# A fused attention and feed-forward kernel: TensorE's run on a pair broken in two places by feed-forward work, the weights' floor on ScalarE and GpSimd, the first values copied out of PSUM, and new orders

## The chip, the cores and the metric

The kernel runs on one core of a Trainium2 chip. The metric is the device time of one execution in microseconds. Three executions of the kernel before took 775.16, 775.26 and 775.63 us (median 775.26).

## What is computed

`reference()` does an attention with a cumulative bias and then a gated feed-forward layer, for 8 batches, 8 heads, 576 positions and a head width of 64:

```
scores = q @ k.T / 8 + min(cum[key] - cum[query], 0)        # cum = cumsum(max(s, 0)); causal
attn   = exp(scores - max);  attn /= sum(attn) + 1e-9
x      = attn @ v, heads side by side                        # 8 x 576 x 512
h      = relu(x @ w_in)                                      # 512 -> 1024
gate   = sigmoid(conv of three taps over positions of h)     # conv_w: 3 x 1024
out    = (h * gate) @ w_out                                  # 1024 -> 512
```

q, k, v and s are 32-bit floats; `w_in`, `conv_w` and `w_out` come as 64-bit floats and are turned into 32-bit ones on the chip, by integer work on their two words.

## The kernel before

**Pairs.** The 64 heads are handled as 32 pairs p, two heads in the two halves of the 128 partitions; four pairs make a batch. A pair's work, by the names of the tasks in the code:

- `qk`, `v`: loads. `hi`, `lo`: the operands are split into a rounded 32-bit part (`hi`, ScalarE or VectorE) and the rest (`lo`, GpSimd or VectorE), so that three products give nearly full precision.
- `sh0` to `sh3` (L1038): a first product of scores on TensorE, in four parts, each into two PSUM banks; `mx` (L1060, L1069): VectorE takes their row maxima. For late pairs (p >= 7) the bias comes through rows `rw` that GpSimd cuts (L996). `tn` (L1089), `rt`, `ds`: the maxima are turned and sent by DMA to the row that serves as shift.
- `sc0` to `sc3` (L1156): the scores proper, four parts, two banks each; `ex` (L1175): ScalarE takes the exponential (by a sigmoid with an offset) out of PSUM into `pt`; `mk` (L1187): GpSimd cuts the diagonal blocks.
- `sum` (L1269): the row sums by a product with ones (from p = 9 on, after additions `ad` on VectorE and GpSimd); `pv` (L1212): the product with the values, into the one PSUM tile `pv` (two banks).
- `gd`, `fo`, `inv`, `ri`, `rb` (L1288 to L1316): the sums are folded over the partitions by a DMA, inverted on VectorE, stored to DRAM and read back spread over the partitions into `rb`. `nm` (L1324): VectorE multiplies the PSUM tile `pv` by `rb`; by that the tile comes free for the next pair's `pv`. `xh`, `xl`: the result is split again and kept as `x`.

**Feed-forward work**, for each batch in two halves of the positions (256 and 320): `h` (L1376, 12 matmuls for each of 8 columns of `w_in`, one bank), `re`, `ce`, `ta`, `tb`, `ga`, `mu` (ScalarE and VectorE), `uh`, `ul` (split into `u`), and `o` (L1505, six matmuls for each fourth of an output block, whose bank is held over the four), `oe`, `st`.

**PSUM** has eight banks: two for `pv` and six (`ps`) for everything else.

**Weights.** `weight_piece` (L742 and on) loads 8 pieces of `w_in` and 4 of `w_out` with 512 columns, 8 of `w_out` with 256, and `conv_w` with 24. The wide ones use three sets of buffers `w` of their own, the others the feed-forward buffers `ht` and `ct`, of which there are three each. A piece goes through these steps: `load`; `one` (L774, VectorE: low part of the high word, shifted); `square` (L781, ScalarE: the square of the high word read as a float, into a buffer of its own); `two` (L785, VectorE: sign and top exponent bit); `both` (L791, VectorE: bits of the low word); `three` (L799, VectorE: multiplies by 0 where the square is too small); `h` and `l`, the split into `wi` or `wo`.

**The order.** All instructions of all engines are put in order on the host before the launch. `Sched.play` simulates the engines with a duration per task (the numbers in `add(...)`), a DMA rate, waits and buffers, and at each moment lets an engine take the ready task with the lowest tag. A tag is a due time from the task's place in the pair plus a number from the table `DUE`. TensorE prefers tasks of the mode that it is in (by 4 us of tag), since a change of mode has a cost in the simulation. The order that comes out is fixed in the program; at run time each engine works it off and waits where something isn't ready. SyncE issues all DMAs.

**Bursts.** From pair 9 (`B0`) on, the TensorE tasks around a pair form a burst: `ORDER` lists them, `group()` gives those that belong together one number, and while a burst is open TensorE takes no other task. In the kernel before, the whole list is one burst: `sh0`, `sh1` of the next pair, `sum`, `pv` of the previous one, `sh2` of the next, `sc0`, `sc1` of this one, `sh3`, `sc2`, `sc3`. `link()` chains the tasks in this order and lets the first task of a part wait for all that its part needs. A "|" in `ORDER` begins a new part.

Of the kernel before, what the change touches and what calls it, by code (L numbers as in the profile page):

```python
# [1623 lines left out]
```

## Time and profile before

| | |
|---|---|
| median of three executions | 775.26 us (775.16 to 775.63) |
| the profiled execution | 780.03 us, of which 778.1 us are its span |
| granted TensorE clock, mean | 0.987 of full speed |
| busy: TensorE, VectorE, ScalarE, GpSimd | 729.7, 568.5, 445.5, 350.4 us |
| DMA | 75.15 MB, mean 97 GB/s |

The span runs from the first to the last instruction. Busy time of TensorE holds the time of a matmul record even where the array waits inside it, and the records overlap; so a stage is better read from the starts of its instructions. The granted clock has two levels here, 1.2 and 2.4 GHz, shown as 0.50 and 1.00 of full speed; a value between them is a stretch that holds both.

### The profile page before, as it was taken

To read this page: it belongs to the slowest core of one execution; us is meant where nothing else is said; L and a number is where in the kernel's file an instruction comes from. 1 tells how busy PE (TensorE), PEld (TensorE's weight loads), DVE (VectorE), ACT (ScalarE), POOL (GpSimd) and SP (SyncE) were. 2 spreads that over 40 slices of the span, in tenths; PEclk is the share of its full clock that TensorE was granted. 3 is DMA by queue.
4 is the path that set the end of the run, shared out by engine and by line. 5 is a ranking of instruction groups with operands and counts; after the bars stand their busy time and mean duration, and the time that the engine had idled before them with its cause. 6 is when DMAs were issued, how large, how long until landed. Compare 5 with 4: busy or idle time off the path is not lost.

```text
span 778.1 us, 19047 instructions
## 1 busy us (share of the span) xinstructions
PE 729.7 (94%) x7200; PEld 605.8 (78%) x7200; DVE 568.5 (73%) x1464; ACT 445.5 (57%) x890; POOL 350.4 (45%) x564
## 2 busy tenths in 40 slices
PE   2688789999999999999989999999999999999998
PEld 2566578787797879887877779887978778788986
DVE  7675688676778787967795777868796858855734
ACT  6455566665565654655654555655666545563534
POOL 6163234522664463426555566345545463642201
PEclk9998999999999999999988999999999999999999
DMA  7752532332323142224322342233324240211010
GB/s 216 225 178 72 188 115 64 100 121 84 112 92 100 54 127 80 67 76 129 115 90 78 112 128 62 70 99 90 133 67 141 81 124 15 81 43 51 14 41 27
DMA packets 50965, 75.15 MB, mean 97 GB/s; under 512 B 14586, under 2 KB 27194, under 8 KB 50874
## 3 DMA queue, kind: packets, MB, share of 16 engines
q1 hardware_dynamic: 50874, 73.94, 30.6%
q8 instruction: 56, 0.92, 0.5%
q14 instruction: 35, 0.29, 0.1%
HBM read 63.58 MB, written 10.03 MB: 95 GB/s over the span
## 4 chain that ended last, share of the span: by engine, by line
PE 77%; DMA 9%; DVE 4%; issue 3%; ACT 2%; POOL 2%; SPq 1%; DVEq 0%; POOLq 0%; ACTq 0%
PE ps L1376 26%; PE ps L1505 25%; PE ps L1156 10%; PE pv L1212 8%; PE ps L1038 4%; PE ps L1269 3%; DMA w<-w_in 2%; DMA rb<-ri_d 2%; DVE ps L1069 2%; DMA ri_d<-rc 1%; DMA rc<-rs 1%; DMA ht<-w_out 1%; ACT pt L1175 1%; POOL rw L996 1%; DVE ct L1414 0%
## 5 line engine op out<-in xcount | busy, mean ns | idle before, releaser
L1376 PE MATMUL ps<-x,wi 128*128 128x258 f32 (+1 forms) x1536 | 216.8, 299 | 0.0
L1376 PEld LDWEIGHTS ps<-x,wi 128*128 128x128 f32 x1536 | 211.9, 190 | 4.2 <-issue 0.2
L1505 PE MATMUL ps<-wo,u 128*128 128x512 f32 x768 | 187.5, 397 | 0.0
L1175 ACT ACTIVATE pt<-ps,less 128x288 f32<-128x288 f32 (+1 forms) x256 | 134.4, 594 | 79.0 <-PE ps L1156 74.9
L1414 DVE SCALAR_TENSOR_TENSOR ct<-ht,cw_sb,ct 128x320 f32<-128x320 f32 (+3 forms) x256 | 144.5, 579 | 45.3 <-ACT ct L1399 42.1
L1505 PEld LDWEIGHTS ps<-wo,u 128*128 128x128 f32 x768 | 140.5, 188 | 31.7
L1156 PE MATMUL ps<-s 64*128 64x288 f32 (+4 forms) x1152 | 120.3, 312 | 12.6 <-ACT pt L1175 5.2
L1069 DVE CUSTOM_DVE_ANT_0 ps<-ps,rw 128x288 f32<-128x288 f32 (+4 forms) x250 | 102.8, 454 | 32.1 <-PE ps L1038 13.6
L996 POOL TENSOR_SCALAR_AFFINE_SELECT rw<-rw 128x256 f32<-128x256 f32 (+1 forms) x125 | 62.9, 512 | 101.5 <-DVE r L1069 59.0
L1156 PEld LDWEIGHTS ps<-s 64*128 64x128 f32 (+1 forms) x1152 | 91.2, 184 | 20.8 <-ACT pt L1175 8.4
L1448 POOL TENSOR_TENSOR u<-ct,u 128x512 fp32r<-128x512 f32 x34 | 46.5, 1370 | 134.1 <-ACT u L1443 128.9
L1187 POOL TENSOR_SCALAR_AFFINE_SELECT pt<-pt 128x128 f32<-128x128 f32 x230 | 81.0, 374 | 50.7 <-ACT pt L1175 48.2
L1212 PE MATMUL pv<-pt,v 128*32 128x448 f32 (+4 forms) x1536 | 95.0, 396 | 5.4 <-DVE rb L1324 5.4
L1387 ACT ACTIVATE ht<-ps 128x257 f32<-128x257 f32 (+1 forms) x128 | 52.7, 413 | 74.5 <-PE ps L1376 72.4
L1212 PEld LDWEIGHTS pv<-pt,v 128*32 128x32 f32 x1536 | 50.1, 112 | 48.3 <-issue 31.9
L1038 PE MATMUL ps<-s 64*128 64x288 f32 (+4 forms) x384 | 62.9, 347 | 8.7 <-DVE s L938 2.4
L944 POOL TENSOR_TENSOR s<-raw,s 128x1152 fp32r<-128x1152 f32 x21 | 56.8, 2703 | 26.8 <-issue 12.3
L1399 ACT ACTIVATE ct<-ht,cw_sb 128x256 f32<-128x256 f32 (+1 forms) x117 | 62.2, 534 | 4.5
L1156 PE MATMUL ps<-eq,ek 64*128 64x288 f32 (+2 forms) x360 | 59.0, 306 | 3.3 <-DMA eq<-rt 3.3
L1428 ACT ACTIVATE ct<-ct 128x640 f32<-128x640 f32 (+1 forms) x64 | 43.6, 682 | 30.4 <-DVE ct L1414 30.2
L1038 PEld LDWEIGHTS ps<-s 64*128 64x128 f32 x384 | 38.0, 195 | 28.1 <-ACT pt L1175 9.7
L1434 DVE TENSOR_TENSOR ct<-ct,ht 128x640 f32<-128x640 f32 (+1 forms) x64 | 50.7, 793 | 11.8 <-ACT ct L1428 11.4
(107 smaller groups left out, 888.1 us busy)
## 6 DMA issues: line engine op xcount, KB each, us to landing
raw<-qk SPq DMA_DIRECT2D x32, 576.0 KB
rw<-cum_d SPq DMA_DIRECT2D x25, 576.0 KB
v<-vp SPq DMA_DIRECT2D x32, 320.0 KB
rb<-ri_d SPq DMA_DIRECT2D x64, 144.0 KB
out<-ob SPq DMA_DIRECT2D x32, 256.0 KB
w<-w_in SPq DMA_DIRECT2D x8, 512.0 KB
ht<-w_out SPq DMA_DIRECT2D x8, 256.0 KB
w<-w_out SPq DMA_DIRECT2D x4, 512.0 KB
```

What stands on the lines that cost most here:

```text
L944: tt_on(e)(st[:, i, :], R_t[raw.slot][:, i], st[:, j, :].bitcast(F32), op=ALU.subtract)
L996: nc.gpsimd.affine_select(out=RW_t[:, :, o : o + k], in_=RW_t[:, :, d : d + k], pattern=[[0, 2], [-1, k]], compare_op=ALU.is_ge, fill=NEG, ...
L1038: nc.tensor.matmul(dst[j], l, m, start=(k == 0), stop=(k == 1 or late))
L1069: nc.vector.tensor_tensor_reduce(out=bank(pb, o, o + c1 - c0), in0=bank(pb, o, o + c1 - c0), in1=add_, scale=1.0, scalar=acc if c0 else -3 ...
L1156: nc.tensor.matmul(d, l, m, start=(k < 2), stop=(k >= len(steps) - 2 or (t == L and k < 2)), skip_group_check=t == L,)
L1175: nc.scalar.activation(PT_t[pts[j].slot][:, o : o + w], bank(pb, 0, w), AF.Sigmoid, bias=less, scale=0.125,)
L1187: nc.gpsimd.affine_select(out=reg, in_=reg, pattern=[[1, dg]], compare_op=ALU.is_ge, fill=0.0, base=0, channel_multiplier=-1,)
L1212: nc.tensor.matmul(pvt[gs, o0 : o0 + c1 - c0], vt[0:jt, t, gs], PT_t[pts[g // 2].slot][0:jt, O_T[t] + c0 : O_T[t] + c1], start=(t == 0), s ...
L1376: nc.tensor.matmul(bank(hb, 0, XW[hf]), l, r, start=(k == 0), stop=(k == len(seq) - 1))
L1399: nc.scalar.activation(o, src, AF.Copy, scale=w)
L1414: nc.vector.scalar_tensor_tensor(cc[:, lo:hi], h_[:, sh + lo : sh + hi], cw_sb[:, 3 * f + k : 3 * f + k + 1], cc[:, lo:hi], op0=ALU.mult, ...
L1505: nc.tensor.matmul(bank(pb, 0, DM), l, r, start=(fp == 0 and k == 0), stop=(fp == NF // 2 - 1 and k == len(seq) - 1),)
```

## The change

- `ORDER` gets two "|", one after `sc0` and one before `sc3`. The list then has three parts, and between two parts TensorE may take feed-forward tasks.
- In `weight_piece` the square and the step `three` are gone. ScalarE takes the absolute value of the high word straight into the result buffer (`size`), a new step `floor` raises it to at least 2^-15 (task `m`: GpSimd, or VectorE), and `one` now works on that in place, so it waits for both. `two` and `both` stay. The buffer for the square goes.
- For the pairs 0 to 4 a new task `vn` (ScalarE, or VectorE at a penalty) copies the values out of the PSUM tile `pv` into a new SBUF buffer `vc`; `nm` then reads `vc`, and the tile comes free after the copy. The memory of `vc` is in the pool that is closed before the first `u`, so that now also waits for `nm` of pair 4.
- The simulation's numbers change: DMA 320 in place of 345 thousand bytes a us, and longer issue times for most DMAs; 0.15 us more for `sc3` of the pairs before 9.
- The whole table `DUE` is replaced, so the order of all engines is another one.

```
-ORDER = ("sh0", "sh1", "sum", "pv", "sh2", "sc0", "sc1", "sh3", "sc2", "sc3")
+ORDER = ("sh0","sh1","sum","pv","sh2","sc0","|","sc1","sh3","sc2","|","sc3")
...
     "pv":
-        "0 -174.1 1 -92.34 2 -59.88 3 -21.85 4 -97.78 5 -26.7 6 -9.52 7 5.91 8 -2.8 9 -15.69 "
+        "0 -16.5 1 -17.89 2 8.8 3 -104.97 4 -8.14 5 -25.48 6 2.78 7 -2.31 8 29.02 9 2.08 10 0.25 "
...
-                    dma_free = max(now + dur + 0.6, dma_free) + t.nbytes / 345e3
+                    dma_free = max(now + dur + 0.6, dma_free) + t.nbytes / 320e3
...
+    vc_t = ep.tile([P, S], F32, name="vc")
...
-        [wp.tile([P, n], F32, name=f"w{i}_{n}{k}") for k, n in enumerate((8 * P, 4 * P, 4 * P))]
+        [wp.tile([P, n], F32, name=f"w{i}_{n}{k}") for k, n in enumerate((8 * P, 4 * P))]
...
+            def size(e):
+                wd, wb = parts()
+                nc.scalar.activation(wb.bitcast(F32), wd[:, :, 1].bitcast(F32), AF.Abs)
+
+            def floor(e):
+                wbf = parts()[1].bitcast(F32)
+                (nc.vector if e == "DVE" else nc.gpsimd).tensor_scalar(
+                    wbf, wbf, 2.0**-15, None, op0=ALU.max,
+                )
+
             def one(e):
-                wd, _, wb = parts()
+                _, wb = parts()
                 nc.vector.tensor_scalar(
-                    wb, wd[:, :, 1], 3, 0x3FFFFFF8, op0=ALU.logical_shift_left,
-                    op1=ALU.bitwise_and,
+                    wb, wb, 3, 0x3FFFFFF8, op0=ALU.logical_shift_left, op1=ALU.bitwise_and,
                 )
-            def square(e):
-                wd, wa, _ = parts()
-                nc.scalar.activation(wa, wd[:, :, 1].bitcast(F32), AF.Square)
...
-            def three(e):
-                _, wa, wb = parts()
-                wbf = wb.bitcast(F32)
-
-                nc.vector.scalar_tensor_tensor(
-                    wbf, wa, 1.2 * 2.0**-30, wbf, op0=ALU.is_ge, op1=ALU.mult
-                )
...
+            tq = add(name + "q", [("ACT", c_act(n) + 0.02)], [t0], tag, size, uses=ws)
+            ta = add(name + "m", [("POOL", 0.19 + n * 0.9e-3, True), ("DVE", 0.13 + n / 1.6e3, True)], [tq], tag,
+                     floor, uses=ws)
+            t1 = add(name + "1", [("DVE", 0.13 + n / 1.6e3, True)], [ta], tag, one, uses=ws)
             t2 = add(name + "2", [("DVE", c_tt(n) + 0.05, True)], [t1], tag, two, uses=ws)
-            t3 = add(name + "b", [("DVE", c_tt(n) + 0.05, True)], [t2], tag, both, uses=ws)
-            last = add(name + "3", [("DVE", c_tt(n) + 0.05, True)], [t3, ta], tag, three, uses=ws)
+            last = add(name + "b", [("DVE", c_tt(n) + 0.05, True)], [t2], tag, both, uses=ws)
...
+        spare = p < 5
+
+        def take(e):
+            copy_on(e)(vc_t, pvt[:, PV0 : PV0 + S])
 
         def norm(e):
-            nc.vector.tensor_tensor(rb_t, pvt[:, PV0 : PV0 + S], rb_t, op=ALU.mult)
-
-        t_norm = add(f"nm{p}", [("DVE", 0.77)], [t_rb, t_pv], tq, norm, uses=[rb, pv])
-        last_nm[:] = [t_norm]
+            nc.vector.tensor_tensor(
+                rb_t, vc_t if spare else pvt[:, PV0 : PV0 + S], rb_t, op=ALU.mult
+            )
+
+        t_free = t_pv
+        if spare:
+            vc = buf("vc")
+            t_free = add(f"vn{p}", [("ACT", c_act(S) + 0.1), ("DVE", 0.77, False, 3.0)], [t_pv], tq, take,
+                         alloc=[vc], uses=[pv])
+        t_norm = add(f"nm{p}", [("DVE", 0.77, spare)], [t_rb, t_free], tq, norm,
+                     uses=[rb, vc if spare else pv])
+        last_nm[:] = [t_free if spare else t_norm]
+        if p == 5 - 1:
+            last_sh.append(t_norm)
```

## Rows read from the trace of the kernel before

**Rows 1.** From the page: its first line, the engines' busy times, and the shares of the chain of work that ended last.

```profile
span 778.1 us, 19047 instructions
...
PE 729.7 (94%) x7200; PEld 605.8 (78%) x7200; DVE 568.5 (73%) x1464; ACT 445.5 (57%) x890; POOL 350.4 (45%) x564
...
PE 77%; DMA 9%; DVE 4%; issue 3%; ACT 2%; POOL 2%; SPq 1%; DVEq 0%; POOLq 0%; ACTq 0%
```

**Rows 2.** Busy time of the engines in three stretches (stretch in us from the span's start: its length, then busy us and instructions of TensorE's matmuls, its weight loads, VectorE, ScalarE, GpSimd, then the granted clock, the DMA share and GB/s): from the first scores to the first feed-forward matmul, from there to the end, and one stretch in the middle.

```profile
29.40:119.50 90.10, 77.44 (x1236) 60.55 (x1236) 64.22 (x168) 48.17 (x102) 35.02 (x26) 0.94 0.47 142
119.50:778.10 658.60, 643.60 (x5904) 539.15 (x5902) 483.64 (x1246) 380.07 (x760) 300.31 (x511) 0.99 0.27 85
400.00:420.00 20.00, 16.94 (x128) 14.88 (x117) 14.61 (x39) 10.82 (x21) 12.67 (x21) 0.74 0.33 94
```

**Rows 3.** The same columns, in stretches of 4 us.

```profile
88.00:92.00 4.00, 2.00 (x20) 0.86 (x24) 2.81 (x9) 2.48 (x6) 0.26 (x1) 0.73 0.14 26
...
404.00:408.00 4.00, 3.62 (x25) 3.34 (x26) 3.99 (x15) 2.31 (x6) 2.65 (x5) 0.50 0.63 144
```

**Rows 4.** From the list of waits: TensorE's `pv` for `nm` on VectorE (us in total, times, longest).

```profile
PE pv L1212 <- DVE rb L1324: 5.4, 2, 3.9
```

**Rows 5.** From the timeline of TensorE (start, us, instruction, idle time before it and what ended it): `pv` of pair 3.

```profile
90.00 4.47 PE L1212 MATMUL pv<-pt,v 128*32 128x128 f32 x48 [3.91 <-DVE rb L1324]
```

**Rows 6.** From the timeline of TensorE: one burst, from `sh0` and `sh1` over the first sums, `pv`, `sc0`, `sc1`, `sh3` and the first matmul of `sc2` to the feed-forward work behind it.

```profile
343.65 0.53 PE L1038 MATMUL ps<-s 64*128 64x288 f32 x4
344.12 0.30 PE L1269 MATMUL ps<-pt,onehot 128*32 128x128 f32 x1
...
344.69 2.87 PE L1212 MATMUL pv<-pt,v 128*32 128x128 f32 x48
...
347.83 0.64 PE L1156 MATMUL ps<-s 64*128 64x288 f32 x6
...
348.43 0.56 PE L1156 MATMUL ps<-s 64*128 64x288 f32 x6
348.82 0.30 PE L1156 MATMUL ps<-eq,ek 64*128 64x288 f32 x2
349.24 0.80 PE L1038 MATMUL ps<-s 64*128 64x320 f32 x3
349.83 0.39 PE L1156 MATMUL ps<-s 64*128 64x448 f32 x1
```

**Rows 7.** From the chain of work that ended last, in order of time (start, us, what): two `o` pieces of six matmuls, the first one right behind a burst.

```profile
213.28 1.60 PE ps L1505 x6
...
214.99 1.39 PE ps L1505 x6
```

**Rows 8.** From the timeline of TensorE, another burst: the end of `sc1`, `sh3`, and the beginning of `sc2`.

```profile
430.30 0.29 PE L1156 MATMUL ps<-eq,ek 64*128 64x288 f32 x2
430.43 0.40 PE L1038 MATMUL ps<-s 64*128 64x320 f32 x4
430.67 1.39 PE L1156 MATMUL ps<-s 64*128 64x448 f32 x6
```

**Rows 9.** The columns of rows 2, one stretch for each of the 23 bursts, from its first matmul to the end of its last `sc3`: the first, a usual one, the longest, the last (which has no `sh` parts), the sum of all 23, and the sum of the seven longest (those that begin at 186.56, 236.79, 276.98, 397.12, 424.12, 458.75 and 568.20).

```profile
186.56:197.96 11.40, 9.95 (x166) 7.92 (x165) 7.59 (x30) 4.59 (x9) 4.02 (x10) 1.00 0.21 63
...
343.65:352.26 8.61, 8.49 (x130) 6.30 (x129) 7.00 (x29) 5.15 (x11) 3.58 (x8) 1.00 0.16 42
...
397.12:411.51 14.39, 11.33 (x130) 8.86 (x129) 12.75 (x38) 7.13 (x16) 9.27 (x15) 0.73 0.20 45
...
692.00:699.19 7.19, 7.07 (x118) 5.21 (x117) 3.28 (x8) 4.94 (x11) 0.89 (x4) 1.00 0.05 7
sum 211.78, PE 200.52 PEld 148.03 DVE 169.16 ACT 112.86 POOL 98.80; mean PE 8.72 PEld 6.44 DVE 7.35 ACT 4.91 POOL 4.30
...
sum 73.98, PE 65.87 PEld 48.82 DVE 59.29 ACT 34.80 POOL 38.10; mean PE 9.41 PEld 6.97 DVE 8.47 ACT 4.97 POOL 5.44
```

**Rows 10.** Groups of instructions by line and shape in the first 120 us (count, busy us, mean ns of one, idle time before): `three` (L799) and `one` (L774) for 512 and 256 columns, and GpSimd's `l` for the same widths.

```profile
L799 DVE SCALAR_TENSOR_TENSOR w<-w,w 128x512 f32<-128x512 f32 x12 | 8.6, 723 | 0.0
L774 DVE TENSOR_SCALAR w<-w 128x512 uint32<-128x512 uint32 x12 | 5.7, 493 | 4.4 <-DMA w<-w_in 4.4
L799 DVE SCALAR_TENSOR_TENSOR ct<-ct 128x256 f32<-128x256 f32 x6 | 2.4, 409 | 0.0
L774 DVE TENSOR_SCALAR ct<-ht 128x256 uint32<-128x256 uint32 x8 | 2.3, 290 | 3.9 <-DMA ht<-w_out 3.9
L837 POOL TENSOR_TENSOR wi<-w,wi 128x512 fp32r<-128x512 f32 x8 | 10.7, 1332 | 14.1 <-ACT wi L834 6.9 <-DMA raw<-qk 4.4 <-DVE wi L834 2.9
L858 POOL TENSOR_TENSOR wo<-ct,wo 128x256 fp32r<-128x256 f32 x6 | 4.6, 775 | 16.1 <-ACT wo L855 16.1
```

**Rows 11.** From the timelines of GpSimd and of VectorE: a step `l` of one weight piece, and the step `both` of another.

```profile
26.68 1.34 POOL L837 TENSOR_TENSOR wi<-w,wi 128x512 fp32r<-128x512 f32 x1 [6.88 <-ACT wi L834]
...
26.81 1.77 DVE L791 SCALAR_TENSOR_TENSOR w<-w,w 128x512 uint32<-128x512 uint32 x1
```

**Rows 12.** From the chain that ended last, in order of time: the last load of narrow pieces of `w_out`, and the first `h`.

```profile
107.27 5.01 DMA ht<-w_out
...
119.55 3.73 PE ps L1376 x24
```

**Rows 13.** From the groups by line and shape: ScalarE's exponential of 512 columns out of PSUM.

```profile
L1175 ACT ACTIVATE pt<-ps,less 128x512 f32<-128x512 f32 x128 | 79.9, 688 | 22.5 <-PE ps L1156 18.5 <-POOL rw L996 1.4 <-POOL u L1448 1.2
```

More of the change, by code (lines that the diff above doesn't have):

```diff
@@ L83 @@
     "x":
-        "s -10.8 clear 31.21 ident 15.44 tab 69.8 hot 16.85 unit 10.12 mrow -31.37 tri -10.31 "
-        "eb 1.66 cum 2.89 rest -10.19 grid 37.88 rst 4.28 tnc 17.5 save 11.27 off 8.79 cw -6.06 "
-        "cwb 1.22 cwh 20.86",
[3 rows of a table added]
     "pads":
-        "0 3.89 1 -28.75 2 -11.99",
+        "0 5.12 1 -3.36 2 -5.57",
     "ind":
[1 row of a table removed]
[1 row of a table added]
     "cw":
[1 row of a table removed]
[1 row of a table added]
     "wi":
[4 rows of a table removed]
[3 rows of a table added]
     "wo":
[7 rows of a table removed]
[5 rows of a table added]
     "qk":
[9 rows of a table removed]
[9 rows of a table added]
     "hi":
[4 rows of a table removed]
[4 rows of a table added]
     "lo":
[4 rows of a table removed]
[4 rows of a table added]
     "dr":
[39 rows of a table removed]
[41 rows of a table added]
     "rw":
[3 rows of a table removed]
[3 rows of a table added]
     "rk":
[14 rows of a table removed]
[12 rows of a table added]
 }
@@ L731 @@
     if RB < NP:
-        t_save = add("save", [("SP", 0.7)], [t_cum, t_ncr], 9.0, save, nbytes=300000)
+        t_save = add("save", [("SP", 1.4)], [t_cum, t_ncr], 9.0, save, nbytes=300000)
     def offsets(e):
@@ L762, in load @@
                 nc.sync.dma_start(
-                    parts()[2].bitcast(F32).rearrange("p (a b) -> p a b", a=split), src
+                    parts()[1].bitcast(F32).rearrange("p (a b) -> p a b", a=split), src
                 )
-            last = add(name, [("SP", 0.4)], wait, tag, load, alloc=ws, nbytes=P * n * 4, prev=prev)
+            last = add(name, [("SP", 0.47)], wait, tag, load, alloc=ws, nbytes=P * n * 4, prev=prev)
         else:
@@ L789, in both @@
             def both(e):
-                wd, _, wb = parts()
+                wd, wb = parts()
                 nc.vector.scalar_tensor_tensor(
@@ L793, in both @@
                 )
-            def three(e):
-                _, wa, wb = parts()
-                wbf = wb.bitcast(F32)
-                nc.vector.scalar_tensor_tensor(
-                    wbf, wa, 1.2 * 2.0**-30, wbf, op0=ALU.is_ge, op1=ALU.mult
-                )
-            t0 = add(name, [("SP", 0.4)], wait, tag, load, alloc=ws, nbytes=P * n * 8, prev=prev)
-            ta = add(name + "q", [("ACT", c_act(n) + 0.02)], [t0], tag, square, uses=ws)
-            t1 = add(name + "1", [("DVE", 0.13 + n / 1.6e3, True)], [t0], tag, one, uses=ws)
+            t0 = add(name, [("SP", 0.47)], wait, tag, load, alloc=ws, nbytes=P * n * 8, prev=prev)
+            tq = add(name + "q", [("ACT", c_act(n) + 0.02)], [t0], tag, size, uses=ws)
+            ta = add(name + "m", [("POOL", 0.19 + n * 0.9e-3, True), ("DVE", 0.13 + n / 1.6e3, True)], [tq], tag,
+                     floor, uses=ws)
+            t1 = add(name + "1", [("DVE", 0.13 + n / 1.6e3, True)], [ta], tag, one, uses=ws)
             t2 = add(name + "2", [("DVE", c_tt(n) + 0.05, True)], [t1], tag, two, uses=ws)
-            t3 = add(name + "b", [("DVE", c_tt(n) + 0.05, True)], [t2], tag, both, uses=ws)
-            last = add(name + "3", [("DVE", c_tt(n) + 0.05, True)], [t3, ta], tag, three, uses=ws)
+            last = add(name + "b", [("DVE", c_tt(n) + 0.05, True)], [t2], tag, both, uses=ws)
         def hi(e):
-            finish_hi(e, parts()[2].bitcast(F32))
+            finish_hi(e, parts()[1].bitcast(F32))
         h = add(name + "h", [("ACT", c_act(n)), ("DVE", c_cp(n), True, 1.0)], [last], tag, hi,
@@ L818, in lo @@
         def lo(e):
-            finish_lo(e, parts()[2].bitcast(F32))
+            finish_lo(e, parts()[1].bitcast(F32))
         return add(name + "l", [("POOL", c_pool(n), True), ("DVE", c_tt(n), True, LO2)], [h], tag,
@@ L926, in load @@
             nc.sync.dma_start(R_t[raw.slot], qk[p])
-        t_load = add(f"qk{p}", [("SP", 0.35)], [], A - QKA, load, alloc=[raw], nbytes=589824)
+        t_load = add(f"qk{p}", [("SP", 0.45)], [], A - QKA, load, alloc=[raw], nbytes=589824)
         def load_v(e):
             nc.sync.dma_start(V_t[vb.slot], vp[p])
-        last_v[0] = t_v = add(f"v{p}", [("SP", 0.4)], [last_v[0], t_eb, t_off, t_tnc, *t_ind, *t_pads], A - 2, load_v,
+        last_v[0] = t_v = add(f"v{p}", [("SP", 0.45)], [last_v[0], t_eb, t_off, t_tnc, *t_ind, *t_pads], A - 2, load_v,
                               alloc=[vb], nbytes=327680)
@@ L964, in pair @@
         last_ek[0] = t_ek = add(
[L965 removed]
+            f"dr{p}", [("SP", 1.3)], [last_ek[0], t_grid, t_rst, *t_pads],
             (A if late else a_sh) - DRA, d_rows, alloc=[ek], nbytes=50000,
@@ L1162, in pair @@
             w = sum(c1 - c0 for _, c0, c1 in part)
-            t_sc = add(f"sc{p}.{i}", [("PE", 4 * c_rt(part, 66) + (0 if p >= B0 else 0.06 * sum(-(-min(P, c1 - c0) // D) for _, c0, c1 in part if c0 == 0)))], [t_mrow, t_shift, t_dr, *t_lo], A + 0.1 * i,
+            t_sc = add(f"sc{p}.{i}", [("PE", 4 * c_rt(part, 66) + (0 if p >= B0 else 0.15 * (i == 3) + 0.06 * sum(-(-min(P, c1 - c0) // D) for _, c0, c1 in part if c0 == 0)))], [t_mrow, t_shift, t_dr, *t_lo], A + 0.1 * i,
                        sc_mm, alloc=pbs + (pts if i == 0 else []), uses=[sb, ek, eq], mode="r",
@@ L1296, in fold @@
                 )
-        t_fold = add(f"fo{p}", [("SP", 0.8)], [t_grd], tq, fold, uses=[ri], nbytes=30000)
+        t_fold = add(f"fo{p}", [("SP", 1.2)], [t_grd], tq, fold, uses=[ri], nbytes=30000)
         def inverse(e):
@@ L1306, in store_ri @@
             nc.sync.dma_start(ri_d.rearrange("j (g k c) -> (j g k) c", g=4, k=16), rc_t)
-        t_ri = add(f"ri{p}", [("SP", 0.36)], [t_inv], tq, store_ri, uses=[ri], nbytes=30000)
+        t_ri = add(f"ri{p}", [("SP", 0.4)], [t_inv], tq, store_ri, uses=[ri], nbytes=30000)
         def spread(e):
```

16 lines of the change are left out of this document (7 added, 9 removed), and 160 rows, old and new, of the table DUE.

## The prediction

> **What bounds the kernel now.** I read the page first: TensorE is busy for 729.7 of the 778.1 us, and 77% of the chain that ended last is TensorE's own work [rows 1]. So a gain has to come out of the 48.4 us in which TensorE has no matmul, or out of waits that hide inside its busy time. Then I read the stretches. From the first scores at 29.4 us to the first feed-forward matmul at 119.5 us TensorE is busy for 77.4 of 90.1 us, at a granted clock of 0.94; from there to the end for 643.6 of 658.6 us [rows 2]. So 12.7 us are open in the front part, 15.0 us behind it, and the rest is the start.
>
> The front part is not TensorE's: VectorE is busy for 64.2 of its 90.1 us (71%), with the weights' steps among its work, and the chain goes through the loads of `w_out` pieces until the first `h` [rows 2, 12]. The largest single wait there is `pv` of pair 3: 3.91 us idle until `nm` has read the tile, and then 4.47 us where a later one takes 2.87, in a stretch whose clock is 0.73, that is, partly at 1.2 GHz [rows 3, 5, 6]. All waits of `pv` for `nm` are 5.4 us, in two places [rows 4].
>
> Behind the front part the waits sit in the bursts, where the page doesn't show them. I read one burst start by start. Between the last two matmuls of `sc1` and `sh3` pass 0.42 us (348.82 to 349.24), and `sh3` takes 0.59 us until `sc2` begins (349.83) [rows 6]. In another burst the same two steps take 0.13 and 0.24 us [rows 8]. So the usual burst waits 0.29 + 0.35 = 0.64 us there, and without it its 8.61 us would be 7.97 [rows 9]. All 23 bursts take 211.78 us; without the last, which has no `sh`, 22 take 204.59. Against 22 x 7.97 = 175.3 that is 29.2 us of waiting: 73.98 - 7 x 7.97 = 18.2 in the seven longest, and 11.1 (0.74 each) in the other fifteen [rows 9]. The worst stands in the stretch from 400 to 420 us, where the clock is 0.74, and 0.50 from 404 to 408 [rows 2, 3].
>
> **The change part by part.** The sums are made against the profiled execution, 780.03 us with its span of 778.1; the median is 4.8 us below it, and I take a saving to be the same in both.
>
> *Breaks.* A break that is used costs a way out and a way back. Out: the first `o` piece behind a burst takes 1.60 us, the next one 1.39, so 0.21 [rows 7]. Back: `sh0` and `sh1`, four matmuls of 288 columns, take 0.47 us (343.65 to 344.12), where eight of the same size take 0.60 inside the burst (347.83 to 348.43), so four are 0.30 and the way back is 0.17 [rows 6]. One break is 0.38 us, two are 0.76, and if all 22 bursts use both, 16.7 us. For it TensorE gets 1.39 us of work that it has to do anyhow, while ScalarE and VectorE empty the banks of `sh2` and `sc0`. The wait that I found stands between `sc1` and `sh3`, inside the middle part, where no break is; but with a piece of 1.39 us ahead of `sc1` those banks are empty 1.8 us later, which is more than the 0.64. For the seven long bursts I take 60% of the 18.2 us as gained, 10.9, less 7 x 0.76 = 5.3: 5.6 us. For the fifteen usual ones I take one break each (5.7 us) and 60% of 11.1 (6.7 us): 1.0 us. Together 6.5 us; from below, all breaks used and nothing gained is 16.7 us lost; from above, all waits gone with two breaks each is 29.2 - 16.7 = 12.5 gained.
>
> *Values copied out.* `pv` of pair 3 then waits for a copy of its predecessor that needs nothing from the DMA chain: the 3.91 us go, and of the 4.47 the 1.60 above 2.87, if TensorE doesn't fall to 1.2 GHz; with the other wait of 5.4 - 3.9 = 1.5 us that is 7.0 [rows 4, 5, 6]. What is late next is the `sh` behind it and VectorE's maxima, and with them the weights, so I take 4, between 0 and 7. The added copies: five of 576 columns, by the exponential of 512 out of PSUM (0.69 us) 0.77 each as an estimate [rows 13], 3.9 us on ScalarE, which is free for 42 of the 90 us [rows 2]. They are hidden; were they not, they would cost those 3.9. `nm` stays one instruction of VectorE.
>
> *Weights.* `three` goes: 12 x 0.723 + 8 x 0.409 = 11.9 us of VectorE [rows 10]. ScalarE's step only changes its function. The floor is shown by no row. If VectorE does it, I price it like `one`, 12 x 0.493 + 8 x 0.290 = 8.2 us, and 3.7 us of VectorE are left as gain. If GpSimd does it, I bound it by its `l`, 12 x 1.332 + 8 x 0.775 = 22.2 us [rows 10], on an engine that is busy for 35 of the 90 us [rows 2]. The chain of a piece gets one hop longer, since `one` now waits for ScalarE and the floor; it is covered where a piece waits in its buffers anyhow, and `two` and `both` queue behind it on VectorE. VectorE's work is only in part on the path, so I take 2.5 us, between 4 gained and 4 lost.
>
> One row speaks against GpSimd: while its `l` ran from 26.68 for 1.34 us, a `both` that began at 26.81 took 1.77 us, where L799, of the same width and kind, takes 0.72 [rows 10, 11]. The Trainium skill (SBUF — State Buffer, "Who interferes with whom") says that a VectorE instruction with two inputs in SBUF and a GpSimd instruction that reads SBUF exclude each other. By that rule, the trace agrees, with 1.05 us of delay; it would turn the 2.5 us into a loss, which is the third rival.
>
> *Orders and the simulation's numbers.* Every queue is ordered anew, SyncE's and GpSimd's among them; nothing in the trace prices it. One more burst like the worst would cost 14.39 - 8.61, some 6 us [rows 9]; a front part without idle time would give 12.7 [rows 2]. I take 0. The close of the early memory waits for `nm` of pair 4 too, which by the place of pair 3 at 90 us comes before the first `h`: nothing.
>
> Sum: 6.5 + 4 + 2.5 = 13.0 us. The profiled time would be 767, the median 775.3 - 13.0 = 762.3.
>
> **The rivals.**
>
> *Slower: breaks that cost and don't help.* TensorE uses both breaks in most bursts, the wait before `sh3` stays since it lies inside a part, and the long bursts keep theirs, which come from late engines and not from banks. Then +16.7, with the front's 6.5 gained: 785.5. It decides from the point where a burst gets back less than 0.76 us. For it: the place of the wait [rows 6]. Against it: TensorE can go on with `sc1` at once where the banks are free, and a break not used costs nothing.
>
> *No change: the wait moves.* VectorE is busy for 169 of the 212 us of the bursts (80%) [rows 9]; feed-forward work in a break brings `re`, `ce` and the taps into the same queues, ahead of the maxima and exponentials. The bursts then give nothing, and the front part still ends with the last narrow pieces of `w_out`, whose load alone takes 5.01 us at 107.27 [rows 12], so that of its gain 1 us stays: 774.3.
>
> *GpSimd holds VectorE up.* If the floor is on GpSimd and shuts VectorE out for the 71% in which that has work, VectorE gets 0.71 x 22.2 - 11.9 = 3.9 us more work instead of less. With 2.5 of them on the path in place of 2.5 gained: 762.3 + 5 = 767.3.
>
> *Much faster.* The front part shrinks to TensorE's busy time (12.7 in place of 6.5) and the seven long bursts lose all their waits (18.2 - 5.3 = 12.9 in place of 5.6): 762.3 - 6.2 - 7.3 = 748.8.
>
> **How the numbers follow.** The forecast has a chance of 0.44, with a range of its own from 752 to 771; the slower rival 0.17, no change 0.14, GpSimd 0.12, much faster 0.13. A measurement of this kernel tells 0.2% from no change, 773.7 to 776.8 us. Faster: 0.44, 0.13, 0.12 and a quarter of the case of no change, less a little for a new bad burst: 0.71. The same: 0.07. Slower: 0.17 and the rest, 0.22. The time is that of the likeliest case, 762. The range goes from 748 to 784: below it lies half of the case much faster (0.06), above it about two thirds of the slower one (0.11).
>
> **What would show it.** The breaks are right if the starts of TensorE show feed-forward pieces between `sc0` and `sc1` and between `sc2` and `sc3`, if the work of a burst without these pieces is near 8.0 + 0.4 to 0.8 us, and if none of the bursts waits over 2 us. The copy is right if no `pv` of a pair below 5 waits for `nm`. The weights are right if VectorE's busy time up to the first `h` falls by 4 to 12 us, and wrong if steps of 0.7 us there take over 1.5 beside the floor. If the first `h` stays at 119.5 us, or the bursts take over 204.6 us with the ways in and out, the forecast is wrong; a new stretch with a clock of 0.5 behind 130 us would show that the order made a stall of its own.

## The result, and the profile after

The changed kernel takes 757.44 us (median of four runs, 757.33 to 757.53) beside 775.21 us before (774.87 to 775.63): a ratio of 0.977, 95% interval 0.9753 to 0.9787, so 17.8 us less. The forecast was 762.0 with a range from 748 to 784. Its profiled execution took 757.48 us.

The page of the changed kernel: span, engines, and the shares of the chain that ended last.

```profile
span 755.7 us, 19031 instructions
...
PE 725.9 (96%) x7200; PEld 597.9 (79%) x7200; DVE 572.6 (76%) x1458; ACT 447.9 (59%) x895; POOL 382.7 (51%) x572
...
PE 90%; DVE 4%; ACT 2%; DMA 2%; issue 1%; SPq 0%; POOL 0%; ACTq 0%; DVEq 0%
```

Against [rows 1] TensorE's share of the chain rose from 77 to 90%, DMA's fell from 9 to 2%. TensorE's busy time is only 3.8 us less; what went is idle time. GpSimd has 32.3 us more to do, VectorE 4.1 more.

The same stretches as in [rows 2], and one up to the changed kernel's first `h` at 98.78 us (before: 119.5), in the columns of rows 2.

```profile
29.40:119.50 90.10, 86.17 (x1339) 68.74 (x1336) 74.54 (x185) 61.95 (x127) 57.05 (x46) 1.00 0.53 164
...
29.40:98.80 69.40, 65.67 (x1092) 51.02 (x1088) 57.94 (x139) 47.63 (x96) 45.51 (x33) 1.00 0.56 173
...
400.00:420.00 20.00, 19.80 (x203) 16.36 (x202) 16.86 (x46) 12.89 (x27) 9.82 (x20) 1.00 0.22 70
```

In the same 90.1 us TensorE is busy for 86.2 instead of 77.4, and its granted clock is 1.00 instead of 0.94. The stretch from 400 to 420 us, which had a clock of 0.74, has 1.00.

**Where the time went.** I split the span where the burst of pair 9 begins: at 184.32 us in a second profile of the kernel before (775.26 us, near its median), at 168.78 after. Up to there both have done the same 192 `h` matmuls, but the kernel before 12 `o` matmuls more, two pieces of about 1.4 us. So the front part gained 15.5 - 2.8 = 12.7 us. From there to the end of TensorE's work pass 585.3 us before and 583.3 after, with those 2.8 us more to do: 4.8 gained. Together 17.5. The first matmuls of that burst, before and after:

```profile
184.32 0.53 PE L1038 MATMUL ps<-s 64*128 64x288 f32 x4
```

```profile
168.78 0.54 PE L1033 MATMUL ps<-s 64*128 64x288 f32 x4
```

**A broken burst.** TensorE's timeline in the changed kernel (start, us, instruction): pair 10, from `sh2` over `sc0`, an `o` piece in the first break, to `sc1` and `sh3`.

```profile
211.91 0.50 PE L1033 MATMUL ps<-s 64*128 64x448 f32 x4
212.24 0.64 PE L1151 MATMUL ps<-s 64*128 64x288 f32 x6
212.72 0.29 PE L1151 MATMUL ps<-eq,ek 64*128 64x288 f32 x2
212.94 1.66 PE L1515 MATMUL ps<-wo,u 128*128 128x512 f32 x6
214.53 0.67 PE L1151 MATMUL ps<-s 64*128 64x288 f32 x6
215.03 0.30 PE L1151 MATMUL ps<-eq,ek 64*128 64x288 f32 x2
215.16 0.40 PE L1033 MATMUL ps<-s 64*128 64x320 f32 x4
```

The piece holds TensorE from 212.94 to 214.53, 1.59 us. Behind it `sc1` and `sh3` run without a gap: 0.13 us lie between the last two matmuls of `sc1` and `sh3`, where [rows 6] had 0.42. In the plan 24 of the 44 breaks are used, 14 behind `sc0` and 10 ahead of `sc3`, with 25 pieces in them.

**All bursts.** For each of the 22 bursts of pairs 9 to 30 I add up its attention work, from its first matmul to the start of what follows its last `sc3`, without the pieces in its breaks: 201.8 us in the second profile of the kernel before, 192.0 after. The seven bursts in which no break is used (pairs 9, 11, 12, 16, 19, 25 and 27) go from 66.4 to 61.7 us, 4.7 less. The fifteen broken ones go from 135.4 to 130.3. All of those 5.1 us are in pair 18 (13.1 to 8.0), which in the order before waited 2.3 us for ScalarE's exponentials and then ran partly at half the clock; the other fourteen together are even. The wait in the second profile of the kernel before:

```profile
402.02 1.09 PE L1156 MATMUL ps<-s 64*128 64x288 f32 x6 [2.31 <-ACT pt L1175]
```

### The profile page after: what moved, and what is told of

It is laid out like the page before. It is cut to its first block, busy times and chain, and to the rows that moved or that the text cites. A ratio compares the mean times of both kernels' runs of the same rounds, so it can differ in the third digit from the quotient of the medians.

```text
span 755.7 us, 19031 instructions
## 1 busy us (share of the span) xinstructions
PE 725.9 (96%) x7200; PEld 597.9 (79%) x7200; DVE 572.6 (76%) x1458; ACT 447.9 (59%) x895; POOL 382.7 (51%) x572
## 4 chain that ended last, share of the span: by engine, by line
PE 90%; DVE 4%; ACT 2%; DMA 2%; issue 1%; SPq 0%; POOL 0%; ACTq 0%; DVEq 0%
PE ps L1386 28%; PE ps L1515 27%; PE ps L1151 14%; PE pv L1207 11%; PE ps L1033 5%; PE ps L1264 4%; DVE r L1055 2%; ACT pt L1170 1%; DMA w<-w_in 1%; PE ps L1084 1%; DMA ht<-w_out 0%; DMA ek<-grid_d 0%; DVE ps L1064 0%; DVE w L793 0%; DMA rc<-rs 0%
## 5 line engine op out<-in xcount | busy, mean ns | idle before, releaser
L1386 PE MATMUL ps<-x,wi 128*128 128x258 f32 (+1 forms) x1536 | 219.1, 299 | 0.0
L1515 PE MATMUL ps<-wo,u 128*128 128x512 f32 x768 | 192.3, 399 | 0.1
L1424 DVE SCALAR_TENSOR_TENSOR ct<-ht,cw_sb,ct 128x256 f32<-128x256 f32 (+3 forms) x256 | 148.5, 599 | 46.8 <-ACT ct L1409 43.9
L1458 POOL TENSOR_TENSOR u<-ct,u 128x512 fp32r<-128x512 f32 x44 | 58.5, 1330 | 145.7 <-ACT u L1453 145.7
L1151 PE MATMUL ps<-s 64*128 64x288 f32 (+4 forms) x1152 | 116.7, 311 | 4.6 <-ACT pt L1170 4.0
L1182 POOL TENSOR_SCALAR_AFFINE_SELECT pt<-pt 128x128 f32<-128x128 f32 x230 | 91.4, 419 | 50.4 <-ACT pt L1170 48.7
L991 POOL TENSOR_SCALAR_AFFINE_SELECT rw<-rw 128x256 f32<-128x256 f32 (+1 forms) x125 | 65.8, 535 | 99.4 <-DVE r L1064 72.3
L1151 PEld LDWEIGHTS ps<-s 64*128 64x128 f32 (+1 forms) x1152 | 84.7, 181 | 18.3 <-ACT pt L1170 8.3
L1033 PE MATMUL ps<-s 64*128 64x288 f32 (+4 forms) x384 | 56.8, 338 | 6.1 <-ACT s L933 1.6
L939 POOL TENSOR_TENSOR s<-raw,s 128x1152 fp32r<-128x1152 f32 x20 | 54.6, 2732 | 7.2 <-DVE s L933 3.2
L1151 PE MATMUL ps<-eq,ek 64*128 64x288 f32 (+2 forms) x360 | 53.4, 303 | 0.0
L1453 ACT CAST u<-ct 128x512 fp32r<-128x512 f32 x62 | 38.3, 618 | 24.8 <-DVE ct L1444 24.3
```

The costliest lines, as they stand in the source:

```text
L991: nc.gpsimd.affine_select(out=RW_t[:, :, o : o + k], in_=RW_t[:, :, d : d + k], pattern=[[0, 2], [-1, k]], compare_op=ALU.is_ge, fill=NEG, ...
L1033: nc.tensor.matmul(dst[j], l, m, start=(k == 0), stop=(k == 1 or late))
L1151: nc.tensor.matmul(d, l, m, start=(k < 2), stop=(k >= len(steps) - 2 or (t == L and k < 2)), skip_group_check=t == L,)
L1182: nc.gpsimd.affine_select(out=reg, in_=reg, pattern=[[1, dg]], compare_op=ALU.is_ge, fill=0.0, base=0, channel_multiplier=-1,)
L1386: nc.tensor.matmul(bank(hb, 0, XW[hf]), l, r, start=(k == 0), stop=(k == len(seq) - 1))
L1424: nc.vector.scalar_tensor_tensor(cc[:, lo:hi], h_[:, sh + lo : sh + hi], cw_sb[:, 3 * f + k : 3 * f + k + 1], cc[:, lo:hi], op0=ALU.mult, ...
```

## The experiments

All kernels but two controls start from the order of tasks that the kernel before or after computes. That order is changed at the named tasks only; the others keep theirs unless an input or a buffer forbids it, and waits follow from it. So a part can be taken out of the new order, or put on the old one, without a new plan. The edits are shown shortened, in names that say what they do.

### The kernel before, once more

> The kernel before once more, for a second profile, since its first profiled execution took 780.0 us where the median of its timed runs is 775.3. If the long burst from 397 to 411 us (14.4 us, with a clock of 0.5) belongs to every execution, it stands here too and the span is near 778. If it is a chance of that execution, the burst takes about 9 us here and the span is near 773, and some 5 us of what the two first profiles differ by are no gain of the change.

It took 775.26 us; 13 other runs of it, on the same chip, spread from 772.0 to 779.9. Its profile, with a span of 773.3 us, keeps the long burst (13.1 us from 394.77), but with only 3.4 us at a clock of 0.50 there, where the first profile had 10.2. So the stretch of [rows 3] varies from run to run: the burst and the `h` behind it took 2.4 us less here. That is half of the 4.8 us between the two profiles; the other half lies in the front part, since the burst of pair 9 begins at 184.32 instead of 186.56.

### One part taken out of the changed kernel

All 25 pieces moved out of the breaks, behind the last `sc` part of their burst:

```
+    for p in range(B0, NP - 1):              # TensorE's tasks from sc0 to sc3
+        for t in pe[index(f"sc{p}.0") : index(f"sc{p}.3")]:
+            if t.name[0] in "ho":
+                place[t] = behind(f"sc{p}.3")
```

> The kernel after, its order kept, but the 25 feed-forward pieces that stand between the score parts of a pair from 9 on are moved behind the last part. Theory 1, the breaks pay: the waits in the bursts come back, at least 0.64 us where a break was and more in some, less 0.38 for each break: 760 to 766 us against 757.4. Theory 2, the breaks cost as much as they give: 756 to 759. Theory 3, the breaks cost more, and the gain came in spite of them: 748 to 755.

Measured: 814.4 us, ratio to before 1.0497 (1.0450 to 1.0544), so some 56 us above the changed kernel by the two ratios, and far above all three theories. Two lines of its list of waits (us in total, times, longest), and the one of them that the changed kernel has:

```profile
PE ps L1151 <- DVE r L1064: 18.9, 15, 2.6
PE ps L1151 <- ACT pt L1170: 12.3, 23, 0.9
```

```profile
PE ps L1151 <- ACT pt L1170: 4.0, 10, 0.6
```

The same two waits are 0 and 4.0 us in the changed kernel. The scores now wait for VectorE's maxima and for ScalarE's exponentials. This doesn't give the worth of a break by itself: with the `h` pieces also their consumers came late, and the other engines' queues stood, but for a few tasks of ScalarE and VectorE, in the order that counted on them. The run of six pieces below leaves those queues as they are.

The copy taken out:

```
             nc.vector.tensor_tensor(
-                rb_t, vc_t if spare else pvt[:, PV0 : PV0 + S], rb_t, op=ALU.mult
+                rb_t, pvt[:, PV0 : PV0 + S], rb_t, op=ALU.mult
             )
+    drop(f"vn{p}" for p in range(5))         # nm frees the PSUM tile again
```

> The kernel after, its order kept, but without the copy: the values of pairs 0 to 4 are multiplied out of PSUM as before, so the next pair's product with the values waits for that. Theory 1, the copy takes away the wait that the prediction named: 761 to 765 us, with waits of TensorE for the multiplication of 4 to 7 us in all. Theory 2, the new order alone had moved that wait away: 757 to 759.

Measured: 770.7 us, ratio 0.9935 (0.9906 to 0.9963). The difference of the two ratios is 0.0165, 12.8 us; by their intervals it is known to within about 3 us. That is the first theory's direction, but some 6 us beyond the time that it gave. TensorE's timeline in this kernel: three `pv` of 48 matmuls, with the idle time before them and what ended it; then a stretch in the columns of rows 2.

```profile
67.87 4.60 PE L1207 MATMUL pv<-pt,v 128*32 128x128 f32 x48 [2.39 <-DVE rb L1324]
...
81.64 2.90 PE L1207 MATMUL pv<-pt,v 128*32 128x128 f32 x48 [1.63 <-DVE rb L1324]
...
116.50 4.59 PE L1207 MATMUL pv<-pt,v 128*32 128x128 f32 x48 [5.75 <-DVE rb L1324]
```

```profile
113.13:119.95 6.83, 3.46 (x28) 1.23 (x32) 4.85 (x16) 0.81 (x2) 1.18 (x2) 0.50 0.27 87
```

Without the copy there are three waits of `pv` for `nm`, 9.8 us, instead of the 5.4 in two places of [rows 4]. Two of them have a second price: TensorE goes on at half the clock, and 48 matmuls take 4.6 instead of 2.9 us. The third alone costs 5.75 + 1.69 us. The first `h` begins at 103.37, 4.6 late, and the burst of pair 9 at 180.87, 12.1 late; behind that nothing changes (583.7 against 583.3 us).

The weights' old steps in the changed kernel:

```
-    size (Abs, ScalarE) -> floor (max 2**-15, GpSimd) -> one -> two -> both
+    one | square (ScalarE) -> two -> both -> three (VectorE)
```

> The kernel after, its order kept, with the weights' old steps: the square on ScalarE, no floor on GpSimd, and the step three on VectorE right behind both. Theory 1, VectorE's time is on the path in the front part: 12 us more of VectorE, 759.5 to 762 us. Theory 2, GpSimd's floor holds VectorE up by as much as the removed step took: 755 to 758.

Measured: 763.8 us, ratio 0.9846 (0.9813 to 0.9879): 0.0076 more than with the new steps, 5.9 us, again to within about 3. The first theory had the direction, with 2 to 4.6 us. Its profiled execution was the slowest of six (768.1); it shows the first `h` at 108.71 and two stretches at a clock of 0.50, 17 us in all, before it. The stretch from 29.4 us to its first `h`, in the columns of rows 2:

```profile
29.40:108.70 79.30, 71.07 (x1091) 54.36 (x1089) 67.51 (x150) 46.92 (x96) 31.24 (x23) 0.89 0.51 153
```

VectorE works 67.5 us there, against 57.9 in the changed kernel's 69.4 us up to its own first `h`: 9.6 us more.

### One part put on the old order

42 feed-forward pieces that followed a burst and whose inputs were ready by the plan's times moved into it, behind `sc0` and ahead of `sc3`:

```
+    for p in range(B0 + 1, NP - 1):
+        place[next_ready_h_or_o()] = behind(f"sc{p}.0")
+        place[next_ready_h_or_o()] = ahead_of(f"sc{p}.3")
```

> The kernel before, its order kept, but 42 feed-forward pieces that were ready are moved from behind a burst into it: one behind sc0 and one behind sc2 of nearly every pair from 10 on. Theory 1, the breaks pay in any order: 767 to 773 us against 775.3. Theory 2, they cost what they give: 773 to 778. Theory 3, 42 breaks at 0.38 us and little gained: 779 to 791.

Measured: 818.0 us, ratio 1.0499 (1.0451 to 1.0546), 39 us slower than the kernel before beside it, 0.9 us for each piece and beyond the third theory. By the pages of this run and of the second profile of the kernel before TensorE is busy for 742.5 us instead of 728.2 and idle for 25 us more; what each piece costs was not taken apart.

The copy, `vn` on ScalarE behind each `pv` of pairs 0 to 4:

```
-            rb_t, pvt[:, PV0 : PV0 + S], rb_t, op=ALU.mult
+            rb_t, vc_t if p < 5 else pvt[:, PV0 : PV0 + S], rb_t, op=ALU.mult
```

> The kernel before, its order kept, with the copy for pairs 0 to 4 put into ScalarE's order where the values are ready. Theory 1: the wait of 3.9 us and the second one of 1.5 go, with the slow stretch behind them: 769 to 772 us. Theory 2: in the old order the next late engine takes the time back, 774 to 775.5.

Measured: 780.2 us, ratio 1.0036 (1.0009 to 1.0062), 2.8 us slower, which is worse than both theories. The waits of `pv` for `nm` are gone from its profile, but the first `h` begins at 120.4, no earlier than before (119.5 and 117.2 in the two profiles).

The new weight steps with every floor on GpSimd:

```
-    one | square (ScalarE) -> two -> both -> three (VectorE)
+    size (Abs, ScalarE) -> floor (max 2**-15, GpSimd) -> one -> two -> both
```

> The kernel before, its order kept, with the new weight steps (absolute value on ScalarE, floor on GpSimd, no step three). Theory 1, VectorE is relieved: 771 to 774 us. Theory 2, the longer chain over three engines and GpSimd's hold on VectorE cost what is gained: 774 to 780.

Measured: 787.7 us, ratio 1.0127 (1.0092 to 1.0163), 10 us slower, beyond both theories; first `h` at 129.0.

All three of these edits together:

> The kernel before, its order kept, with all three edits. If the parts make the gain: 757 to 766 us. If the new order of all engines makes it: 770 us or more, and the rest to 757.4 is the order's.

Measured: 825.9 us, ratio 1.0614 (1.0582 to 1.0645). So no part gains anything on the old order. My reading is that `pv` of pair 3 may start earlier there, but TensorE's next instructions are where they were in its queue, and wait for what they waited for. By it a part that takes a wait away is worth what the order can put in its place.

### The changed kernel beside its last three variants

> The changed kernel once more, as the measure for the three runs beside it, and to see how steady it is. I expect 757.4 us within 0.3, while the kernel before, on the same chip, spreads over several us as it did beside the other runs (772.0 to 781.1). If the changed kernel spreads like that too, the steady times of its first four executions were chance.

Measured, on a third chip: 758.3 us (757.0 to 761.5), ratio 0.9751 (0.9719 to 0.9783), beside 778.3 before (775.2 to 782.2). The spread of 4.5 us is more than I expected; the calm of the first four runs was partly chance.

Copy and new weight steps undone at once, order and breaks kept (the two edits above together):

> The changed kernel's order and breaks, but with the values read out of PSUM by the multiplication as before (no copy) and with the weights' old steps: both undone at once. Alone they cost 13.3 us (770.72 against 757.44) and 6.4 us (763.82). Theory A, each removes a wait of its own: the two add up, 777 us, so that breaks and new order without the two give nothing against the kernel before. Rival B, both hide the same lateness of the front part, so the larger one alone decides: 771 to 773 us, and 3 to 6 us of the gain are then left to breaks and order. I expect B, nearer to A: 774.

Measured: 778.8 us, ratio 1.0003 (0.9979 to 1.0027). The two add up: 20.5 us above the changed kernel on this chip, against 12.8 + 5.9 = 18.7 alone. Theory A holds and the rival, with my own guess of 774, falls. The split at pair 9 says more. Its burst begins at 186.77 us here:

```profile
186.77 0.54 PE L1041 MATMUL ps<-s 64*128 64x288 f32 x4
```

In the kernel before it begins at 184.32 in the second profile and 186.56 in the first, at 181.5 or 183.8 if the two `o` pieces are taken off. So the new order without its two aids makes the front part 3 to 5 us longer than the old one had it. Behind it pass 583.5 us, as in the changed kernel: the 4.8 us there are from breaks and order alone.

Six of the 25 pieces moved out of their breaks, all `o` pieces for which no consumer is in a hurry; all other engines keep their order:

```
+    for t in ("o2.0.0.0", "o3.1.0.1", "o3.1.0.2", "o4.0.0.0", "o3.1.1.1", "o5.0.0.1"):
+        place[t] = behind(last sc part of its burst)     # pairs 14, 20, 20, 21, 21, 26
```

> The changed kernel with six of its 25 feed-forward pieces in breaks (all six are o pieces whose consumers are late anyhow) moved behind the last sc part of their burst; every other engine's order is the same. By my price of a break (0.38 us out and back) and no wait behind it, six breaks less give 2.3 us back: 755.2. By the rival, that TensorE waits there for banks as long as before (0.64 us a burst and more), closing them costs 6 x 0.26 = 1.6 us: 759. In the first case sc1, sh3 and sc2 of these bursts take no longer than in the bursts that are broken; in the second there are new waits in them.

Measured: 771.4 us (764.3 to 773.9), ratio 0.9894 (0.9853 to 0.9936), 13 us slower than the changed kernel beside it. I had expected 755 by one theory and 759 by the other. In its profile (772.2 us span, the slowest of the six runs) the burst of pair 9 begins 4.7 us later, in a part where the two programs are the same, so that much is the run's own; from there to the end it takes 595.0 instead of 583.3 us, 11.8 more for six pieces.

The burst of pair 20 shows why. First the changed kernel, TensorE from its first matmul, then from the end of `sc0`:

```profile
425.18 0.53 PE L1033 MATMUL ps<-s 64*128 64x288 f32 x4
...
429.82 0.29 PE L1151 MATMUL ps<-eq,ek 64*128 64x288 f32 x2
430.05 1.66 PE L1515 MATMUL ps<-wo,u 128*128 128x512 f32 x6
431.63 0.82 PE L1151 MATMUL ps<-s 64*128 64x288 f32 x6
...
433.11 0.89 PE L1151 MATMUL ps<-s 64*128 64x448 f32 x6 [0.28 <-ACT pt L1170]
...
434.35 1.65 PE L1515 MATMUL ps<-wo,u 128*128 128x512 f32 x6
435.93 0.71 PE L1151 MATMUL ps<-s 64*128 64x320 f32 x6
...
437.14 0.29 PE L1084 MATMUL ps<-ident,r 128*32 128x128 f32 x1
```

The same with both pieces moved out, and two of its rows of VectorE:

```profile
431.37 0.53 PE L1033 MATMUL ps<-s 64*128 64x288 f32 x4
...
436.01 0.29 PE L1151 MATMUL ps<-eq,ek 64*128 64x288 f32 x2
437.81 0.84 PE L1151 MATMUL ps<-s 64*128 64x288 f32 x6 [1.50 <-DVE r L1064]
...
439.29 1.49 PE L1151 MATMUL ps<-s 64*128 64x448 f32 x6 [0.28 <-ACT pt L1170]
...
442.40 1.17 PE L1151 MATMUL ps<-s 64*128 64x320 f32 x6 [0.86 <-ACT pt L1170]
...
444.57 1.64 PE L1515 MATMUL ps<-wo,u 128*128 128x512 f32 x3
```

```profile
436.16 0.22 DVE L1296 RECIPROCAL rc<-rc 128x9 f32<-128x9 f32 x1 [2.53 <-DMA rc<-rs]
436.30 0.63 DVE L1064 CUSTOM_DVE_ANT_0 ps<-ps,rw 128x448 f32<-128x448 f32 x1
```

`sc1` begins 6.45 us behind the burst's start with the piece ahead of it (431.63 - 425.18), and 6.44 without (437.81 - 431.37). The first piece costs this burst nothing at all: TensorE would have idled. What it waits for are the maxima of `sh2` on VectorE, and they stand in VectorE's queue behind the reciprocal of the previous pair's sums, which waits 2.53 us for a DMA. Then the second price comes: from 439.25 to 446.08 the clock is 0.50, and the first six matmuls of `sc2` take 1.49 instead of 0.89 us.

```profile
439.25:446.08 6.83, 5.93 (x36) 5.16 (x37) 3.00 (x10) 3.00 (x6) 3.29 (x9) 0.50 0.42 136
```

Without its pieces this burst works 13.2 us instead of 4.87 + 2.72 + 1.21 = 8.8. Pair 21 lost its clock as well (6.8 us from 466.6) and works 13.6 instead of 9.5. Where the clock stayed at 1.00, less was lost: without a piece of 1.59 us the attention work of pair 14 grew by 1.37 us (8.18 to 9.55), without one of 1.58 that of pair 26 by 0.84 (8.84 to 9.68). So a piece is hidden as far as the wait at its place goes, wholly at the first place in pair 20, nearly so in pair 14, by half in pair 26. These four bursts hold 10.7 of the 11.8 us.

All floors on VectorE, at the same places of the order:

```
+    for t in tasks_named("floor"):
+        t.eng = "DVE"                        # 19 of 21 were on GpSimd
```

> The changed kernel with all floors of the weights on VectorE, at the places in its queue where the plan had them on GpSimd. 19 floors leave GpSimd, where they took about 25 us; VectorE gets 11 x 0.55 + 8 x 0.29 = 8.4 us more. Theory: the floor on GpSimd shuts VectorE out for less than that, so the kernel gets slower, by up to the 8.4 us and by 2 to 4 since VectorE isn't always the last: 760 to 761, with the first h later than 98.78 by as much. Rival: GpSimd's floor held VectorE up by more than 8.4 us (a step of 0.43 us took up to 1.48 beside it), so the kernel gets faster: 753 to 756, with a first h before 98.8.

Measured: 759.2 us (756.5 to 761.8), ratio 0.9755 (0.9722 to 0.9787), the same as the changed kernel beside it: neither theory. Groups by line and shape up to 120 us, first of the changed kernel, then of this one (count, busy us, mean ns):

```profile
L775 POOL TENSOR_SCALAR w<-w 128x512 f32<-128x512 f32 x11 | 19.0, 1726 | 5.7 <-ACT w L771 5.7
L793 DVE SCALAR_TENSOR_TENSOR w<-w,w 128x512 uint32<-128x512 uint32 x12 | 8.7, 726 | 0.0
...
L781 DVE TENSOR_SCALAR w<-w 128x512 uint32<-128x512 uint32 x12 | 7.0, 600 | 2.5 <-POOL w L775 2.4
L775 POOL TENSOR_SCALAR ct<-ct 128x256 f32<-128x256 f32 x7 | 6.9, 989 | 3.8 <-ACT ct L771 3.8
...
L1321 ACT COPY vc<-pv 128x576 f32<-128x576 f32 x5 | 3.2, 639 | 4.6 <-PE pv L1207 4.6
```

```profile
L793 DVE SCALAR_TENSOR_TENSOR w<-w,w 128x512 uint32<-128x512 uint32 x12 | 8.2, 684 | 0.0
L775 DVE TENSOR_SCALAR w<-w 128x512 f32<-128x512 f32 x12 | 6.1, 515 | 0.7 <-ACT w L771 0.7
...
L781 DVE TENSOR_SCALAR w<-w 128x512 uint32<-128x512 uint32 x12 | 5.3, 461 | 0.0
...
L775 DVE TENSOR_SCALAR ct<-ct 128x256 f32<-128x256 f32 x8 | 2.3, 290 | 0.9 <-ACT ct L771 0.8
```

19 floors came to VectorE, 11 x 0.515 + 7 x 0.290 = 7.7 us and a small one of 24 columns. Yet VectorE's busy time up to 119.5 us went only from 97.99 to 99.68 us, 1.7 more. Its other instructions became 6 us shorter: L781 falls from 600 to 461 ns. GpSimd's floors no longer lie beside them, which I take as the cause: in the changed kernel a step `one` of 512 columns took 0.42 to 0.84 us beside a floor, and 0.37 to 0.43 with nothing of GpSimd's beside it. The longest of them, 1.48 us from 20.21, which the rival above puts beside the floor, lay beside a split of `s` on GpSimd (L939, 18.79 to 21.41). GpSimd falls from 78.42 to 53.52 us. The first `h` begins at 98.34 us instead of 98.78.

## Why the prediction was right, term by term

| term | predicted | measured |
|---|---|---|
| breaks (with the order behind pair 9) | 6.5 | 4.8, from the split at pair 9; breaks and order not told apart |
| copy | 4 | 12.8, from the kernel without it |
| weights | 2.5 | 5.9, from the kernel with the old steps |
| orders, front part | 0 | 3 to 5 lost, from the kernel without both |
| sum | 13.0 | 18.5 to 20.5, measured as one: 17.8 |

The sign and the range held, and so did the reading of the front part as the place where other engines hold TensorE. The forecast of 762.3 is 4.9 us above the measured 757.44, and that it came so near is in part luck: the copy and the weights were taken 12 us too small together, and the loss of the new order in the front part, taken as 0, cancels some of it. The measured terms of copy and weights are known to within about 3 us each.

*Copy: mis-sized, 4 for 12.8.* The step priced the two waits of the old order. It asked what the removed wait costs where it stands. But the tile is what keeps `pv` and everything behind it from running ahead; the new order, made for the copy, runs further ahead, and there the missing copy costs three waits, 9.8 us together, and stretches at half the clock around two of them, where 48 matmuls take 1.7 us longer each time: 13.2 us, near the 12.8. On the old order the copy was worth -2.8. The copies themselves took 0.64 us each, where I estimated 0.77.

*Orders: 0 was wrong.* "Nothing in the trace prices it" is true, but the term isn't separate from the others. The kernel with order and breaks alone is no faster than before (ratio 1.0003), and the parts on the old order are slower than before; only together do they give 17.8 us. What the three weigh on their own can't be said, therefore; the table gives what each is worth beside the others.

*Breaks: near in size by luck, since the gain lies elsewhere.* The way out is confirmed: an `o` piece in a break takes 1.59 us (212.94 to 214.53), one behind another 1.37. The seven long bursts did give most, 72.2 to 62.5 us, near the 10.9 that I took; but four of them (pairs 9, 11, 19 and 25) have no piece in a break, so no break inside them shortened them. The fifteen usual ones gave nothing (129.6 and 129.5), where I took 6.7. Counted by use, the broken bursts work 5.1 us less and pay 24 x 0.21 = 5.0 for their ways out by the estimate, and the unbroken ones work 4.7 less, about the whole of the 4.8. This doesn't make the breaks worthless: in the order that was made with them, six pieces less cost 11.8 us. No run has the new order planned without breaks, so how much they are worth stays open. The six closed breaks also show that a piece is hidden as far as TensorE waits at its place anyhow, which my price left out. I had placed the wait between `sc1` and `sh3` and in the banks of `sh2` and `sc0`; in pair 20 it stands ahead of `sc1`, and the maxima of `sh2` end it. Of the bursts broken once four work 8.0 us (4.87 + 3.11 for pair 10), less than the forecast's 8.4 to 8.8, and the two others 8.6 and 9.6; unbroken ones take 8.5 to 9.6.

*Weights: mis-sized, 2.5 for 5.9.* VectorE's busy time up to the first `h` fell from 84.9 to 81.4 us, less than the 4 to 12 that I wanted to see. The sign against it didn't come either: no step of 0.7 us took over 1.5, the longest took 1.13. What gained wasn't the floor's place, since either engine gives the same time. In the new order the old steps cost VectorE 9.6 us more between 29.4 us and the first `h`, in one profile, the slowest of that kernel; that these, with `three` at the end of each piece, make up the 5.9 us fits, but no run shows it by itself.

**The rivals.** *Slower breaks* falls by its time, no wait over 0.6 us is left in the bursts, and a break that isn't used costs nothing seen: two bursts without a piece (pairs 12 and 16) take 8.5 us as before. Its core, that a burst gets back no more than it pays, holds for fourteen of the fifteen broken bursts taken together. *No change* falls with the first `h` at 98.8. *GpSimd holds VectorE up* is half right: the hold is there, about 6 us of VectorE's time for 26 us of floors (the rival took 15.8 for 22.2), but VectorE saved the 7.7 of the floors for it, so the sum is nothing, not 5 lost. The Trainium skill (SBUF — State Buffer, "Who interferes with whom") has the two engines shut each other out of a shared pair of ports; that VectorE's other steps shrink by 6 us once the floors leave GpSimd agrees with it. *Much faster*, 748.8, asked for 12.7 us in the front part and got just that; its 12.9 us from the long bursts didn't come.

## What to carry to other kernels

A removed wait is worth what the order behind it can move up: price it in the order that the change brings, or say that the old trace only gives a lower bound. Work put at the place where an in-order engine waits for others is free as far as that wait goes, price of the change of mode included; look in the other engine's queue for what its answer stands behind. Before a gain is credited to a new device, look at the places where the device isn't used: here the bursts without a piece gained as much as the whole stage. And count a stall of TensorE together with the clock behind it.
